# Reordering the loads, the weight conversions and the splits around the first groups of a fused attention and feed-forward kernel

## The chip, the cores and the metric

One core of one Trainium2 chip runs the whole program. The metric is the device time of one execution in microseconds (us), the median over repeated executions.

## The reference, cut to what matters

```python
# r, k, v, w: (4, 8, 768, 48) fp32; u: (8, 48); moe weights arrive as 64-bit floats
for t in range(S):                       # linear attention, a decaying state of 48x48 per batch and head
    cur = u * kt (x) vt
    y[:, :, t] = rt . (state + cur)
    state = wt * state + kt (x) vt
x = y.transpose(0, 2, 1, 3).reshape(3072, 384)
h = max(x @ w1, x @ w2, x @ w3)          # 384 -> 768, elementwise maximum of three products
out = h @ w_out                          # 768 -> 384
```

## The kernel before, in words

**Attention.** The 768 steps of each of the 4 batches are cut in 6 chunks of 128 steps, 24 chunks in all, k = 0 to 23, worked in order with all 8 heads together. Each chunk runs through steps that a letter names: `n` loads its transposed inputs (tile `tin`, three buffers), `b` and `f` are two scans on VectorE, `r` three multiplications on VectorE, `d` and `D` and `e` make the diagonal term (for chunks from 6 on `d` is two GpSimd multiplications and a VectorE sum; `e` ends in two GpSimd selects), `X` is the scores on TensorE, `M` the masked copy of the scores by VectorE, `T`, `R`, `U`, `V`, `Z` are small TensorE stages, `S` the new state, `c` a check on ScalarE (a square, summed), `E` copies the result to `x` and, at the third and fourth chunk of a half, issues DMAs inside SBUF that move 16 rows (`x<-x`, L570). X, V, U and Z of a chunk come together; the text calls that stretch on TensorE the chunk's visit. V needs M of the same chunk.

**Layer.** The 3072 tokens are six halves of 512. Half h takes chunks 4h to 4h+3. A half has 18 groups, here G0 to G17 for the first half (three matrices times six column blocks of 128), and then eight out-steps, out0 to out7. In the first half, G0 to G5 multiply in plain fp32 (one term); from G6 on each product is split in a high and a low part, three matmul terms for each of three row blocks: `x_hi*wh`, `x_lo*wh`, `x_hi*wl`. So G6 and on need the split of x (`x_hi` by ScalarE, then `x_lo` by VectorE) and the split of their weight (`wh` by ScalarE, then `wl` by VectorE). The out-steps of the first half are plain fp32. The product of a group lies in one of three PSUM buffers (`psm`) until it is taken up: by a ScalarE copy (L132) for the first of three matrices, by a VectorE maximum (L135) for the other two. G0 and G1 are begun on the first three chunks' columns and ended on the fourth's.

**Weights.** There are 24 weight blocks of 128 rows, 0 to 17 for the groups, 18 to 23 for the second product. A block i goes through: a load by SP's queue into a ring of six `raw` buffers (`load_w`); a cast on ScalarE (`split_w1`, tile `top`, L311); a VectorE instruction that joins the halves to fp32 (`split_w2`, L318); and the split of it (`split_w3`: `wh` on ScalarE L112, and `wl` on VectorE L113, issued one call of `fix` later). A load into a `raw` buffer waits until the VectorE instruction that read the block six before it is over.

**Order.** The schedule is written out by hand: every engine works its instructions in the order in which this code issues them. `FRONT` is a list of steps for chunks 0 to 4 (two characters: a step and its chunk; one character: an action). `START` goes on with actions alone, and then a loop does the rest: there `group()` issues the next group and `unit()` the next sixth of a chunk's visit. The actions: `w` load the next weight block, `i` cast the next one, `c` cast ahead and join the next one (`weights`), `f` split the next one in `ORDER` (6 to 17, then 0 to 5, then 18 to 23) and issue the `wl` of the one before it (`fix`), `y` split the next third of x (`x_next`), `p` and `m` the next group, `a` the next unit of attention. `W3` stands for three idle matmuls. `begin` also loads ahead, up to `NST` blocks past the one being cast.

Of the kernel before, what the change touches and what calls it, by code (L numbers as in the profile page):

```python
# [62 lines left out]
GPH = 3 * FT + 2 * CPH  # L63
UPC = 6
UPH = UPC * CPH
NST = 3
WARM = 10
XD, LEAD = -2, 0

FRONT = ("b0 s0 f0 d0 W2 D0 W3 r0 X0 e0 T0 W3 c0 b1 s1 d1 D1 U0 f1 W2 R0 e1 S0 O0 V0 Z0 E0 n3 r1 "
# [3 lines left out]
TURN = "b1 d1 w | f1 w | D1 r1 c1 | e1 M0 w | "  # L76
ORD = "w R0 V0 U0 X1 Z0 E0 N1 b2 d2 | f2 n3 w | D2 S0 r2 c2 | e2 M1 w | T1 w | |"


START = ("mcyamcyfamcyffamcfamcfamcfaamcfamcfaamcfamcfaamcfamcfaamcfamccaamccamcaaamfamfmfamxfamamfmamf")  # L80
CS = 6
EARLY = 2
LINE = 128
# [12 lines left out]
def kernel(ctx: ExitStack, tc, tin, nat, u_flat, u_pair, v_t, w_all, out, ytr):  # L96
# [13 lines left out]
    def split(hi, lo, src, later=None):  # L110

        nc.scalar.copy(out=hi, in_=src)  # L112
        rest = lambda: nc.vector.tensor_tensor(out=lo, in0=src, in1=hi.bitcast(F32), op=ALU.subtract)  # L113
        rest() if later is None else later.append(rest)
# [90 lines left out]
    with ExitStack() as fast:  # L205
# [88 lines left out]
        def load_w():  # L294
            nonlocal loaded
            if loaded == NW:
                return
            i, loaded = loaded, loaded + 1
            if w_all.dtype == F32:
                place(i)  # L300
                nc.sync.dma_start(out=wval[i], in_=w_all[i])
                return
            raw = raw_p.tile([128, lines(2 * PC + 1)], I32, name="raw")
            nc.sync.dma_start(out=raw[:, :].bitcast(U16)[:, 1:4 * PC + 1], in_=w_all[i].bitcast(U16))
            stage[i] = raw
# [7 lines left out]
        def split_w2(i):  # L313

            if w_all.dtype == F32:
                return
            place(i)
            nc.vector.scalar_tensor_tensor(out=wval[i].bitcast(U32), in0=stage.pop(i)[:, 1:2 * PC:2].bitcast(U32), scalar=13,  # L318
                                           in1=tops[i % 3][:, :], op0=ALU.logical_shift_right, op1=ALU.bitwise_or)
# [12 lines left out]
        def split_w3(i):  # L332

            whi[i] = hi_p.tile([128, PC], F32R, name="wh")[:, :]
            wlo[i] = lo_p.tile([128, PC], F32R, name="wl")[:, :]
            split(whi[i], wlo[i], wval[i], wrest)
# [240 lines left out]
        def ahead(step, k):  # L577

            if k < NK and (step, k) not in ready:
                ready.add((step, k))  # L580
                steps[step](k)
# [63 lines left out]
        def begin():  # L645

            nonlocal begun
            while loaded < min(NW, begun + (NST if groups else 1)):
                load_w()
            if begun < NW:  # L650
                split_w1(begun)
                begun += 1

        def weights():

            nonlocal done
            if done == NW:
                return
            while begun < min(NW, done + 2):
                begin()  # L660
            split_w2(done)
            done += 1

        ORDER = [*range(3 * SPLIT, 3 * FT), *range(3 * SPLIT), *range(3 * FT, NW)]
# [10 lines left out]
        def fix():  # L675

            nonlocal fixed
            flush_one = wrest.pop(0) if wrest else None
            if fixed < NW:
                split_w3(ORDER[fixed])  # L680
            if flush_one:
                flush_one()
            fixed += 1
# [46 lines left out]
        def group():  # L730
# [25 lines left out]
            while fixed < due(half, g):  # L756
                fix()
# [8 lines left out]
        def part():  # L766
# [3 lines left out]
            next(mg)  # L770

        simple = dict(p=part, a=unit, c=weights, i=begin, w=load_w, m=group, f=fix, y=x_next, x=lambda: take_x(True))
        for step in FRONT.split():
            if step in simple:
# [3 lines left out]
            else:  # L778
                ahead(step[0], int(step[1:]))
        for step in START:  # L780
            simple[step]()
# [7 lines left out]
    with tc.If(verdict[0] != 0, label="general"), ExitStack() as slow:  # L789
        pool = lambda name, bufs, **kw: slow.enter_context(tc.tile_pool(name=name, bufs=bufs, **kw))  # L790
        c1 = pool("c1", 1)
# [83 lines left out]
        with tc.For_i(0, NH) as half:  # L875
            x = xs_p.tile([128, KT, HT], F32, name="x")
# [73 lines left out]
```

## Time and profile before

| | |
|---|---|
| median of 3 runs | 412.01 us (411.22 to 412.81) |
| the profiled execution, its own time | 415.78 us |
| its span in the trace | 414.0 us |
| mean granted TensorE clock | 0.984 of full |
| busy: TensorE / VectorE / ScalarE / GpSimd | 397.9 / 253.6 / 177.9 / 82.7 us |

All times in the trace are microseconds from the start of the span, in the profiled execution. An engine name in a row is PE (TensorE), DVE (VectorE), ACT (ScalarE), POOL (GpSimd) or SP; a trailing q is the engine's queue of DMA issues. In a timeline row the first number is the start, the second the duration (of all that a row merges), and what stands in brackets is how long the engine was idle ahead of it and what ended that. Durations of neighbouring instructions on an engine overlap by about a tenth of a microsecond, so the time that one takes in a queue is read from start to start. A plain fp32 matmul leaves two records, so six records are one plain group.

### The profile page before, as it was taken

Reading aid. Unit: us, or ns where it says so; the run is one execution under the profiler, and the core shown is the slowest. Engines: PE = TensorE matmul, PEld = TensorE weight load, DVE = VectorE, ACT = ScalarE, POOL = GpSimd, SP = SyncE. Lnnn points to the kernel's source line nnn. Section 1 sums busy time; section 2 is a strip of 40 time slices with the busy share of each in tenths; the row PEclk is TensorE's granted clock in tenths of the full one; section 3 lists DMA queues with packets and bytes.
Section 4 is the critical chain, followed back from the end, with each engine's and each line's share of the span. In section 5 each row is a group of like instructions: output and inputs, shape, how many; then the busy total and the mean of one; then the engine's idle time right before and its main releaser. Section 6 shows DMA issues by size and latency. Waiting matters only on the chain.

```text
span 414.0 us, 9214 instructions
## 1 busy us (share of the span) xinstructions
PE 397.9 (96%) x3762; PEld 322.8 (78%) x3762; DVE 253.6 (61%) x440; ACT 177.9 (43%) x403; POOL 82.7 (20%) x95
## 2 busy tenths in 40 slices
PE   6997999798999999999999999999999999999995
PEld 2665467675688888988888988889988888978895
DVE  7975789979737858457658558667656532233320
ACT  2854465454524323546545746644623421412211
POOL 3220013235221421311321311322222200000000
PEclk9998799989999999999999999999999999999998
DMA  8766974760540412380330370430460000300002
GB/s 214 210 180 200 351 240 143 246 195 9 175 161 5 126 31 96 74 273 4 123 96 30 81 268 2 149 101 0 141 206 2 2 2 0 97 1 2 1 0 80
DMA packets 20814, 44.65 MB, mean 108 GB/s; under 512 B 2944, under 2 KB 9536, under 8 KB 20768
## 3 DMA queue, kind: packets, MB, share of 16 engines
q1 hardware_dynamic: 20160, 43.34, 33.8%
q10 hardware_dynamic: 608, 0.69, 0.5%
q8 instruction: 30, 0.49, 0.5%
q14 instruction: 16, 0.13, 0.1%
HBM read 38.12 MB, written 4.72 MB: 103 GB/s over the span
## 4 chain that ended last, share of the span: by engine, by line
PE 88%; DVE 4%; ACT 2%; DMA 2%; issue 2%; ACTq 1%; SPq 1%; POOL 0%; POOLq 0%; DVEq 0%
PE psm L169 51%; PE psm L189 19%; PE gram L451 4%; PE y L543 4%; PE tu L504 3%; PE y L494 3%; PE psm L594 2%; PE tu L481 2%; DMA raw<-in_w_all_dram 2%; DVE wl L113 1%; DVE gf L355 1%; PE psm L406 1%; DVE h_hi L135 1%; ACTq L570 1%; SPq L570 1%
## 5 line engine op out<-in xcount | busy, mean ns | idle before, releaser
L169 PE MATMUL psm<-x_hi,wh 128*128 128x512 f32 x306 | 122.6, 401 | 2.1 <-ACT h_hi L132 2.1
L169 PE MATMUL psm<-x_hi,wl 128*128 128x512 f32 x306 | 120.1, 393 | 0.1
L169 PE MATMUL psm<-x_lo,wh 128*128 128x512 f32 x306 | 119.8, 392 | 0.0
L135 DVE TENSOR_TENSOR m<-psm,m 128x512 f32<-128x512 f32 x60 | 41.5, 691 | 72.8 <-PE psm L169 59.9
L169 PEld LDWEIGHTS psm<-x_hi,wh 128*128 128x128 f32 x306 | 57.6, 188 | 14.9 <-ACT h_hi L132 2.3
L169 PEld LDWEIGHTS psm<-x_hi,wl 128*128 128x128 f32 x306 | 57.7, 189 | 13.0 <-DVE wl L113 0.8
L169 PEld LDWEIGHTS psm<-x_lo,wh 128*128 128x128 f32 x306 | 57.8, 189 | 11.4 <-DVE x_lo L113 0.2
L430 POOL TENSOR_SCALAR_AFFINE_SELECT a<-cs 64x512 f32<-64x512 f32 x44 | 31.4, 714 | 135.3 <-DVE cs L421 62.9
L189 PE MATMUL psm<-wl,h_hi 128*128 128x384 f32 x168 | 56.2, 379 | 0.0
L396 POOL TENSOR_TENSOR kr<-kr 128x384 f32<-128x384 f32 x18 | 25.2, 1399 | 108.5 <-PE y L543 100.4
L561 ACT COPY x<-y 112x512 f32<-112x512 f32 x24 | 14.0, 584 | 67.8 <-PE y L543 67.8
L189 PE MATMUL psm<-wh,h_hi 128*128 128x384 f32 x120 | 41.0, 342 | 0.0
L189 PE MATMUL psm<-wh,h_lo 128*128 128x384 f32 x120 | 40.3, 335 | 0.0
L112 ACT CAST h_hi<-m 128x512 fp32r<-128x512 f32 x30 | 18.7, 622 | 47.8 <-DVE m L135 47.8
L189 PEld LDWEIGHTS psm<-wl,h_hi 128*128 128x128 f32 x168 | 31.5, 188 | 5.9
L385 ACT ACTIVATE gf<-gf 112x1034 f32<-112x1034 f32 x24 | 25.6, 1067 | 20.6 <-DVE tin L380 20.6
L113 DVE TENSOR_TENSOR h_lo<-m,h_hi 128x512 fp32r<-128x512 f32 x30 | 20.7, 690 | 21.8 <-ACT h_hi L112 21.8
L368 DVE TENSOR_TENSOR_SCAN gf<-tin,d_fwd 112x517 f32<-112x517 f32 x24 | 33.2, 1382 | 0.7
L355 DVE TENSOR_TENSOR_SCAN gf<-tin,d_bwd 112x517 f32<-112x517 f32 x24 | 30.2, 1260 | 2.8 <-DMA tin<-in_tin_dram 2.8
L543 PE MATMUL y<-a,v 64*48 64x64 f32 (+3 forms) x768 | 25.4, 248 | 2.6 <-issue 1.9
L543 PEld LDWEIGHTS y<-a,v 64*64 64x64 f32 (+1 forms) x768 | 21.4, 128 | 6.3 <-issue 4.5
L132 ACT COPY m<-psm 128x512 f32<-128x512 f32 x30 | 17.4, 581 | 18.6 <-PE psm L169 12.8
(87 smaller groups left out, 500.2 us busy)
## 6 DMA issues: line engine op xcount, KB each, us to landing
tin<-in_tin_dram SPq DMA_DIRECT2D x23, 448.0 KB, 4.6
raw<-in_w_all_dram SPq DMA_DIRECT2D x24, 384.0 KB, 4.6
kr<-in_nat_dram SPq DMA_DIRECT2D x18, 384.0 KB, 4.8
tin<-in_tin_dram SPq DMA_DIRECT2D x23, 231.0 KB, 3.0
v<-in_nat_dram SPq DMA_DIRECT2D x24, 192.0 KB, 4.6
out_dram<-m SPq DMA_DIRECT2D x23, 192.0 KB, 2.1
x<-x SPq DMA_DIRECT2D x30, 32.0 KB, 2.0
tin<-in_tin_dram SPq DMA_DIRECT2D x1, 256.0 KB, 4.5
```

The source lines that it names most:

```text
L112: nc.scalar.copy(out=hi, in_=src)
L113: rest = lambda: nc.vector.tensor_tensor(out=lo, in0=src, in1=hi.bitcast(F32), op=ALU.subtract)
L132: nc.scalar.copy(out=top["m"][:, :], in_=ps[:, :])
L135: nc.vector.tensor_tensor(out=m[:, :], in0=ps[:, :], in1=m[:, :], op=ALU.max)
L169: nc.tensor.matmul(ps[:, :], lhsT=wt[f * 3 + wi][:, ct * 128:(ct + 1) * 128], rhs=xt[:, ct, :], start=(n == 0), stop=(n == KT * len(terms) ...
L189: nc.tensor.matmul(pss[tt][:, 0:DM], lhsT=ht[f][:, tok], rhs=wt[FT * 3 + f][:, :], start=(f == 0 and i == 0), stop=(f == FT - 1 and i == l ...
L355: nc.vector.tensor_tensor_scan(out=gf[0:112, 0, ::-1], data0=t[0:112, 0:WC][:, ::-1], data1=d_bwd[0:112, ::-1], initial=0.0, op0=ALU.mult, ...
L368: nc.vector.tensor_tensor_scan(out=gf[0:112, 1, :], data0=tbuf[k % NB][0:112, 0:WC], data1=d_fwd[0:112, :], initial=0.0, op0=ALU.mult, op1 ...
L385: nc.scalar.activation(out=flat, in_=flat, func=AF.Square, accum_out=acc[0:112, k:k + 1])
L396: nc.gpsimd.tensor_tensor(out=n[:, 0, :], in0=n[:, 0, :], in1=n[:, 1, :], op=ALU.mult)
L430: nc.gpsimd.affine_select(out=a[rows, 0:2, :, :], pattern=[[0, 2], [0, 4], [1, HC]], in_=cs[rows, :].rearrange("p (a b) -> p a b", a=2).un ...
L543: mm = nc.tensor.matmul(p["y"][64 * half:64 * half + m, hh, j, HC * late:C], lhsT=natt[k][0][lo:lo + HC, h * D:h * D + m], rhs=a[:, j, :] ...
```

## The change

It rewrites `FRONT` from the second line on and `START`, sets `NST` from 3 to 5, and lets `fix` join the weight block that it splits where that isn't done yet.

```diff
-NST = 3
+NST = 5
...
-         "W1 X1 d2 D2 e2 w w T1 c1 b2 s2 R1 U1 S1 O1 V1 Z1 E1 f2 r2 "
-         "W4 X2 d3 D3 e3 w n4 w T2 c2 b3 s3 R2 U2 S2 i i O2 V2 Z2 E2 f3 r3 "
-         "W3 X3 T3 i R3 O3 x V3 Z3 E3 w w n5 U3 p p d4 w c n6 w m D4 b4 s4 c c3 S3 m w f4 c e4 m r4 c X4 N4 T4 R4 c4 w w")
+         "W1 X1 d2 D2 e2 w w w w T1 c1 b2 s2 R1 U1 S1 O1 V1 Z1 E1 f2 r2 "
+         "W4 X2 d3 D3 e3 n4 w w T2 c2 b3 s3 R2 U2 S2 i i O2 V2 Z2 E2 f3 r3 "
+         "W3 X3 T3 i R3 O3 x V3 Z3 E3 U3 p p d4 c n5 w w m D4 b4 s4 c3 S3 y c w w m f4 e4 y c m r4 y c f X4 N4 T4 R4 c4 w w n6")
...
-START = ("mcyamcyfamcyffamcfamcfamcfaamcfamcfaamcfamcfaamcfamcfaamcfamccaamccamcaaamfamfmfamxfamamfmamf")
+START = ("mcfamcfamcfamcfamcfaamcfaamcfamcfaamcfamcfaamcfamccaamccamcaamfamfamfamxfmamfmamf")
...
             if fixed < NW:
+                while done <= ORDER[fixed]:
+                    weights()
                 split_w3(ORDER[fixed])
```

Read out, block by block: weight blocks 2 and 3 are loaded two blocks earlier in SP's order, blocks 4 and 5 ahead of the DMAs `x<-x` of chunks 2 and 3 instead of behind them; the loads of `tin` for chunks 5 and 6 come later among the weights. ScalarE casts block 4 after the check and the state of chunk 3 instead of before. x's three splits and the join of blocks 5 to 7 are issued between G0 and G3 instead of from G3 to G6, and the split of each weight from block 6 on about one group earlier. The visits of chunks 5 and 6 come after G10 and G14 (before: after G11 and G15), that of chunk 7 after out1 (before: after out0). The `wl` of block 17 is issued on VectorE behind M of chunk 7, just ahead of G17 (before: between G15 and G16, ahead of the scans of chunk 8). x's splits for the second half are issued at out2, ahead of the check of chunk 9 (before: at out4, behind it). From G1 of the second half on the order is the one of before.

## Rows read from the trace of the kernel before

**Rows 1.** PE's timeline from the end of G1 to the end of G5.
```profile
36.46 0.94 PE L157 MATMUL psm<-x,wh 128*128 128x128 f32 x6
40.07 5.49 PE L169 MATMUL psm<-x,wh 128*128 128x512 f32 x6 [2.67 <-ACT h_hi L132]
45.49 1.14 PE L451 MATMUL gram<-tin 48*64 48x128 f32 x32
...
47.68 7.99 PE L169 MATMUL psm<-x,wh 128*128 128x512 f32 x18
```
**Rows 2.** Windows: busy of PE, PEld, DVE, ACT, POOL, then granted clock, DMA share, GB/s.
```profile
40.00:42.00 2.00, 1.93 (x3) 0.90 (x4) 1.95 (x3) 0.57 (x3) 1.31 (x2) 0.50 1.08 289
...
84.00:85.00 1.00, 1.00 (x4) 0.81 (x3) 1.00 (x3) 0.78 (x3) 0.00 (x0) 0.50 0.00 0
```
**Rows 3.** ACT's timeline from 33 to 40 us.
```profile
33.78 0.62 ACT L311 CAST top<-raw 128x384 f16<-128x384 bf16 x1 [2.60 <-DMA x<-x]
...
37.14 0.62 ACT L311 CAST top<-raw 128x384 f16<-128x384 bf16 x1 [2.69 <-DMA raw<-in_w_all_dram]
37.64 1.05 ACT L385 ACTIVATE gf<-gf 112x1034 f32<-112x1034 f32 x1
...
39.42 0.60 ACT L132 COPY h_hi<-psm 128x512 f32<-128x512 f32 x1
```
**Rows 4.** The timeline of SP's queue in the same stretch.
```profile
26.91 6.58 SPq L570 DMA_DIRECT2D x<-x  x6
33.54 1.05 SPq L304 DMA_DIRECT2D raw<-in_w_all_dram  x2
```
**Rows 5.** One window: from `r` of chunk 4 to `M` of chunk 7 on DVE.
```profile
40.66:97.84 57.18, 53.28 (x470) 36.03 (x468) 48.90 (x84) 29.84 (x64) 14.03 (x15) 0.92 0.66 217
```
**Rows 6.** DVE's timeline: single instructions out of that window.
```profile
42.28 0.68 DVE L380 TENSOR_TENSOR tin<-tin,gf 112x512 f32<-112x512 f32 x1
...
73.54 1.36 DVE L113 TENSOR_TENSOR wl<-wl,wh 128x384 fp32r<-128x384 f32 x1
74.82 2.04 DVE L355 TENSOR_TENSOR_SCAN gf<-tin,d_bwd 112x517 f32<-112x517 f32 x1
...
77.84 0.55 DVE L113 TENSOR_TENSOR wl<-wl,wh 128x384 fp32r<-128x384 f32 x1
...
86.27 1.22 DVE L355 TENSOR_TENSOR_SCAN gf<-tin,d_bwd 112x517 f32<-112x517 f32 x1
...
97.21 0.72 DVE L466 COPY_PREDICATED a<-mask,gram 128x512 f32<-128x512 int32 x1
```
**Rows 7.** POOL's timeline: the `d` multiplications of chunks 7 and 8.
```profile
73.11 1.38 POOL L396 TENSOR_TENSOR kr<-kr 128x384 f32<-128x384 f32 x1 [0.96 <-PE y L543]
74.56 1.21 POOL L397 TENSOR_TENSOR kr<-kr,u_bc 128x384 f32<-128x384 f32 x1
...
87.44 1.37 POOL L396 TENSOR_TENSOR kr<-kr 128x384 f32<-128x384 f32 x1 [3.50 <-PE y L543]
```
**Rows 8.** PE's timeline from G15 to the second half's first group.
```profile
82.78 0.50 PE L169 MATMUL psm<-x_hi,wh 128*128 128x512 f32 x1 [2.07 <-ACT h_hi L132]
...
86.26 0.89 PE L543 MATMUL y<-a,v 64*64 64x128 f32 x16
...
93.06 2.10 PE L189 MATMUL psm<-wl,h_hi 128*128 128x384 f32 x6
...
98.02 0.56 PE L543 MATMUL y<-a,v 64*64 64x128 f32 x16 [1.89 <-issue]
...
100.27 9.94 PE L189 MATMUL psm<-wl,h_hi 128*128 128x384 f32 x30
...
114.02 0.69 PE L169 MATMUL psm<-x_hi,wh 128*128 128x512 f32 x1
```
**Rows 9.** The chain that ended last: start, length, what; the stretch after 114 us.
```profile
367.87 28.81 PE psm L169 x126
```
**Rows 10.** SP's queue: the DMAs `x<-x` after chunk 7.
```profile
101.03 4.04 SPq L570 DMA_DIRECT2D x<-x  x6
```

More of the change, by code (lines that the diff above doesn't have):

```diff
@@ L72 @@
 FRONT = ("b0 s0 f0 d0 W2 D0 W3 r0 X0 e0 T0 W3 c0 b1 s1 d1 D1 U0 f1 W2 R0 e1 S0 O0 V0 Z0 E0 n3 r1 "
[3 rows of a table removed]
[3 rows of a table added]
 TURN = "b1 d1 w | f1 w | D1 r1 c1 | e1 M0 w | "
 ORD = "w R0 V0 U0 X1 Z0 E0 N1 b2 d2 | f2 n3 w | D2 S0 r2 c2 | e2 M1 w | T1 w | |"
-START = ("mcyamcyfamcyffamcfamcfamcfaamcfamcfaamcfamcfaamcfamcfaamcfamccaamccamcaaamfamfmfamxfamamfmamf")
+START = ("mcfamcfamcfamcfamcfamcfaamcfamcfaamcfamcfaamcfamcfaamcfamccaamccamcaamfamfamfamxfmamfmamf")
 CS = 6
```

## The prediction

> **What bounds the kernel now.** I read the chain of waits first. From the second half's first group, at 114.0 us, to the end it is TensorE at one rate: 126 matmuls in 28.81 us, 0.229 each [rows 9]. The change doesn't reorder that stretch, so what it is worth is how much earlier the first matmul of half 1 starts than 114.02 [rows 8]. Ahead of it the timeline of TensorE shows where time is lost; the reader is to look for idle time in brackets, and for a group that takes twice its usual time.
>
> First loss: G1 ends at 37.40 and G2 starts at 40.07, 2.67 us idle, and takes 5.49 us; G3 to G5, same shape, take 7.99, 2.66 each [rows 1]. In the window at 40 us the granted clock is 0.50, 1.2 GHz, in place of 2.4 [rows 2]. So this place costs 2.7 + 2.8. ScalarE's timeline says why: G2 needs the copy at 39.42, which stands behind the check and the state of chunk 3, and those behind the cast of block 4 at 37.14, which waited 2.69 us for its load [rows 3]. SP's queue says why the load was late: it was issued at 33.54, behind six x DMAs that waited for chunks 2 and 3 [rows 4].
>
> Second loss: 2.07 us idle ahead of G15 at 82.78, after which its nine matmuls take 3.48 us (to 86.26) instead of 2.06 [rows 8], clock again 0.50 [rows 2]. Third: 1.89 us ahead of V of chunk 7 at 98.02 [rows 8], which needs M of chunk 7, ended at 97.84 on VectorE [rows 5, 6]. Both come from one engine: between 40.66 and 97.84 VectorE is busy 48.90 of 57.18 us [rows 5]. It is the second bound of this stretch, and its 8.3 us idle is nearly as much as TensorE loses.
>
> **The change part by part.** *Loads of blocks 2 to 5 earlier.* The number of DMAs is the same. Blocks 4 and 5 leave SP's queue before the six x DMAs start at 26.91 [rows 4], so the 2.69 us wait for the load [rows 3] goes. ScalarE's own order then is: cast of block 3 at 33.78 as before, to 34.4 with a small copy; check and state of chunk 3, 1.8 (37.64 to 39.42 before), to 36.2; the new x_hi, 0.5, to 36.7; cast of block 4, 0.5 (37.14 to 37.64), to 37.2; the copy for G2, 0.5, to 37.7 [rows 3]. G2 starts at 37.8 rather than 40.07, idle 0.4, and I expect the clock to stay up, since no gap of that size is followed by 0.50 in these rows; if it falls, 2.8 more (5.49 less 2.66 [rows 1]). x_hi and its x_lo go into time that both engines wait in now: nothing, as long as the copy isn't late. `NST` 5 makes SP wait for the buffer ring at blocks 10 and 13, with chunk 6's inputs behind block 13; that wait ends with the join of block 7 near 44, and the scan that needs those inputs comes past 55: nothing.
>
> *What is late next.* After the copy VectorE takes up G1 (0.6) and starts `r` of chunk 4 at 38.5, not 40.66. It takes 2.2 (to the end of the row at 42.28 [rows 6]), so X of chunk 4 starts near 40.7; X, T, R take 2.2 as from 45.49 to 47.68 [rows 1], and G3 starts at 42.9: 4.8 us ahead. TensorE then has the same work as before from 47.68 to the gap before G15 (80.71), 33.0 us, and chunk 6's visit and G15, G16 behind it, 2.25 (98.02 to 100.27 [rows 8]) and 18 matmuls of 0.229 [rows 9], 4.1: it would reach G17 at about 82.3.
>
> *VectorE's queue.* Its work from `r` of chunk 4 to the `wl` of block 17 is what it did in the window, 48.90 [rows 5], with these differences: one x_lo is done earlier, 0.6 (start to end of a like row, 42.28 [rows 6]); taking up G16 now comes later, 0.6; and the `d` of chunk 8 on GpSimd, which ran from 87.44 [rows 7] where VectorE stood idle, now falls where VectorE is busy. The price of that is read at chunk 7: GpSimd's two instructions at 73.11 and 74.56 [rows 7], and under them a `wl` of 1.36 beside 0.55 alone, and a scan of 2.04 beside 1.22 [rows 6]: 1.6 together. Sum 48.9 - 0.6 - 0.6 + 1.6 = 49.3, and with no idle time left the `wl` of block 17 ends at 38.5 + 49.3 = 87.8. The change puts it behind M of chunk 7; G17's third matmul needs it. So TensorE stands from 82.3 or so to 87.8, over 5 us: the stalls at G2, G15 and V of chunk 7 are gone and a longer one comes at G17. For `d` of chunk 8 nothing is the lower bound (it may meet instructions that it doesn't hold up: end at 86.2). The upper one is all of 1.38 + 1.21 [rows 7], and I add 0.5 for idle time that remains on VectorE: 89.3. I take 1.6, the one pair of rows where it is seen.
>
> The Trainium skill, "SBUF — State Buffer", section "Who interferes with whom", says that a VectorE instruction with two SBUF inputs and a GpSimd instruction that reads SBUF contend, and that the later one waits until the first is over. Rows 6 and 7 agree that they contend, with 0.8 us for each in place of a whole GpSimd instruction. By the rule this visit costs up to 2.6 instead of 1.6, and the saving below would be 1.8 instead of 2.8; it speaks against putting VectorE's idle time to use under GpSimd.
>
> *From G17 on.* Seven matmuls remain, 1.6 [rows 9]. A stall of 5 us is longer than either that was followed by a clock of 0.50, so I charge a fall: 1.7 as at G15 (3.48 less 2.06, and V's 0.82 less about 0.5 [rows 8]) to 2.8 as at G2 [rows 1], taken as 2.3. Then T, R and the visit of chunk 7 and the eight out-steps: from out0 at 93.06 to 114.02 less the 1.89 idle, 19.1 [rows 8]. Moving the visit behind out1 changes only the order. x's splits for half 1 now stand on ScalarE ahead of the copy of the first output tile, and they wait for the DMAs that take SP 4.04 us to issue [rows 10]. I estimate that the copy comes 7.4 us after the visit, where TensorE needs its buffer after four steps of the visit's successors at about 7.0: 0.4, between 0 and 1.6.
>
> *Sum.* 87.8 + 1.6 + 2.3 + 19.1 + 0.4 = 111.2 for the first matmul of half 1, against 114.0: 2.8 us saved. On the profiled execution's own 415.8 (span 414.0 and 1.8 around it) that is 413.0; the median shown is 3.8 lower, so 412.0 - 2.8 = 409.2. With the bounds: 86.2 + 1.6 + 1.7 + 19.1 = 108.6, 5.4 saved, to 89.3 + 1.6 + 2.8 + 19.1 + 1.6 = 114.4, 0.4 lost: 406.6 to 412.4.
>
> **The rivals.** *All of it comes back.* If VectorE's queue isn't what holds G17 (its work being shorter than the window's sum, or the `wl` early enough), G17 ends at 84.4 and half 1 starts at 84.4 + 19.1 + 0.4 = 103.9: 10 saved, 402. For it: 8.3 us of VectorE's idle time in the window, and TensorE's losses add up to about that. Against it: the sum of the queue, in which 5 us would have to be missing. With half of them missing it is 405.
>
> *The early part doesn't come off.* Either the loads don't land sooner, or the clock falls at G2 all the same. G2 at half rate delays G3 to G5 by 2.8, VectorE waits for them, and G17 with it: 2.8 - 2.5, about 412, no change. For it: the DMA engines' share is 1.08 at 40 us [rows 2], though that is where these loads leave from; and the gap before G2 still is 0.4.
>
> *Slower.* GpSimd holds VectorE up longer. 14.03 us of GpSimd work lie in the window [rows 5]. If each of the three `d` visits, all now under a busy VectorE, cost the whole 2.6, and the selects as much as they last, the `wl` of block 17 would end at 93 or later. From 92.7 on (4.9 past 87.8) the kernel is more than 0.5% slower: about 414.5 at 93. Against it: in the same rows the contention is 1.6 for a whole visit, and it is in the 48.9 for two of the three.
>
> **How the numbers follow.** My forecast has 0.61, the whole or half of the gain 0.13, no early gain 0.18, slower 0.08. 0.5% is 2.1 us, about what a measurement of this kernel can tell from no change. Of the forecast, two thirds lie beyond 2.1 us saved (0.41) and the rest within it (0.20). So faster is 0.41 + 0.13 = 0.54, same 0.20 + 0.18 = 0.38, slower 0.08. The likeliest time is 409.2, its own range 406.6 to 412.4. The range that holds 8 in 10 goes to 404.0, halfway into the first rival, and to 413.0, so as to hold the second: left out are about 0.08 below and 0.08 above.
>
> **What would show it.** ScalarE's cast of block 4 without a wait for its load; G2 at about 37.8 and in 2.7 us; X of chunk 4 near 41 and G3 near 43; no idle time before G15 beyond 1 us and none before V of chunk 7; VectorE without idle time from 38.5 to 88; and then G17 split in two, two matmuls before and seven after a gap of some 5 us that ends with the `wl` of block 17 near 87.8, clock 0.50 behind it. I am wrong if that gap is missing (then the gain is over 5 us), if G2 still runs at 1.2 GHz, or if the stretch from out0 to half 1 holds a new wait of over 2 us.

## The result, and the profile after

The changed kernel takes 407.3 us (median of 4 runs, 406.0 to 408.1) against 412.4 of the kernel before (411.2 to 413.5) beside it: ratio 0.9874, 95% interval 0.9835 to 0.9913. A second measurement later gave 406.8 against 412.7, 0.9868 (0.982 to 0.9915). The span of the profiled execution fell from 414.0 to 406.4 us.

**A correction first.** The `START` in the section on the change is not that of the kernel that ran. In copying it two pieces `mcfa` were lost, and the reading of the order behind it and the prediction went by the short one. The right line is:

```diff
+START = ("mcfamcfamcfamcfamcfamcfaamcfamcfaamcfamcfaamcfamcfaamcfamccaamccamcaamfamfamfamxfmamfmamf")
```

By it the visits of chunks 5 and 6 stay behind G11 and G15, as before; the `wl` of block 17 is issued between G14 and G15, three groups ahead of M of chunk 7, which stands behind G17; and x's splits for the second half stay at out4. What was said of `FRONT`, of `NST`, of `fix` and of chunk 7's visit behind out1 holds. The order that the prediction reasoned about was run as a kernel of its own, below.

TensorE's timeline after, which answers to [rows 1, 8]:

```profile
37.97 2.84 PE L169 MATMUL psm<-x,wh 128*128 128x512 f32 x6 [0.18 <-ACT h_hi L132]
...
42.69 7.99 PE L169 MATMUL psm<-x,wh 128*128 128x512 f32 x18
...
76.75 0.50 PE L169 MATMUL psm<-x_hi,wh 128*128 128x512 f32 x1 [1.89 <-ACT h_hi L132]
...
80.57 0.56 PE L543 MATMUL y<-a,v 64*64 64x128 f32 x16
...
87.03 2.10 PE L189 MATMUL psm<-wl,h_hi 128*128 128x384 f32 x6
...
91.97 0.56 PE L543 MATMUL y<-a,v 64*64 64x128 f32 x16
...
106.25 0.47 PE L169 MATMUL psm<-x_hi,wh 128*128 128x512 f32 x1
```

G2 waits 0.18 us instead of 2.67 and takes 2.84 instead of 5.49. The gap before G15 is still there, 1.89 us. V of chunk 7, at 91.97, has no idle time ahead of it. Half 1 starts at 106.25 instead of 114.02, 7.8 us earlier, and the rest of the span is as long as before (300.2 and 300.0 us).

Windows after (columns as in [rows 2]): the clock stays at 1.00 where it was 0.50 at 40 us, and is again below 1 behind G15's gap.

```profile
40.00:44.00 4.00, 4.00 (x57) 2.25 (x56) 4.00 (x8) 3.13 (x6) 0.00 (x0) 1.00 1.04 398
76.00:80.00 4.00, 3.25 (x8) 2.57 (x9) 4.00 (x8) 3.82 (x10) 1.31 (x2) 0.64 0.87 262
```

ScalarE after, against [rows 3], and further down the check of chunk 7:

```profile
36.81 0.66 ACT L311 CAST top<-raw 128x384 f16<-128x384 bf16 x1
37.31 0.60 ACT L132 COPY h_hi<-psm 128x512 f32<-128x512 f32 x1
...
75.06 1.07 ACT L385 ACTIVATE gf<-gf 112x1034 f32<-112x1034 f32 x1 [2.63 <-DVE tin L380]
...
76.12 0.57 ACT L132 COPY h_hi<-psm 128x512 f32<-128x512 f32 x1
```

The cast of block 4 (36.81) doesn't wait, and G2's copy follows at once. The last two rows explain G15's gap: the copy that frees a product buffer stands behind the check of chunk 7, which waited 2.63 us for VectorE's `r` of chunk 7.

VectorE after, which answers to [rows 6]:

```profile
38.64 1.21 DVE L379 TENSOR_TENSOR tin<-tin,gf 112x256 f32<-112x256 f32 x2
...
78.23 0.55 DVE L113 TENSOR_TENSOR wl<-wl,wh 128x384 fp32r<-128x384 f32 x1
...
84.98 0.56 DVE L318 SCALAR_TENSOR_TENSOR wl<-raw,top 128x384 uint32<-128x384 uint32 x1 [3.07 <-ACT top L311]
...
91.15 0.72 DVE L466 COPY_PREDICATED a<-mask,gram 128x512 f32<-128x512 int32 x1
```

`r` of chunk 4 starts at 38.64 (40.66 before), the `wl` of block 17 is over at 78.7, and M of chunk 7 (91.15) just in time for V at 91.97.

### The profile page after: what moved, and what is told of

Same layout as the page of the kernel before. It is cut to its first block, busy times and chain, and to the rows that moved or that the text cites. A ratio compares the mean times of both kernels' runs of the same rounds, so it can differ in the third digit from the quotient of the medians.

```text
span 406.4 us, 9216 instructions
## 1 busy us (share of the span) xinstructions
PE 394.4 (97%) x3762; PEld 322.2 (79%) x3762; DVE 252.9 (62%) x440; ACT 177.9 (44%) x403; POOL 79.7 (20%) x95
## 4 chain that ended last, share of the span: by engine, by line
PE 88%; DVE 4%; ACT 2%; issue 2%; ACTq 1%; DMA 1%; POOL 0%; SPq 0%; POOLq 0%; DVEq 0%
PE psm L169 51%; PE psm L189 19%; PE gram L451 4%; PE y L543 4%; PE tu L504 3%; PE y L494 3%; PE psm L594 2%; PE tu L481 2%; ACTq L570 1%; DVE wl L113 1%; DMA v<-in_nat_dram 1%; PE psm L406 1%; DVE gf L368 1%; DVE h_hi L135 1%; DVE gf L355 0%
## 5 line engine op out<-in xcount | busy, mean ns | idle before, releaser
L396 POOL TENSOR_TENSOR kr<-kr 128x384 f32<-128x384 f32 x18 | 23.5, 1308 | 108.1 <-PE y L543 100.7
L355 DVE TENSOR_TENSOR_SCAN gf<-tin,d_bwd 112x517 f32<-112x517 f32 x24 | 31.1, 1295 | 3.3 <-DMA tin<-in_tin_dram 3.3
L132 ACT COPY m<-psm 128x512 f32<-128x512 f32 x30 | 17.4, 581 | 19.2 <-PE psm L169 14.6
L113 DVE TENSOR_TENSOR x_lo<-x,x_hi 128x512 fp32r<-128x512 f32 x18 | 11.5, 688 | 21.4 <-ACT x_hi L112 21.4
```

The source lines that it names most:

```text
L132: nc.scalar.copy(out=top["m"][:, :], in_=ps[:, :])
L355: nc.vector.tensor_tensor_scan(out=gf[0:112, 0, ::-1], data0=t[0:112, 0:WC][:, ::-1], data1=d_bwd[0:112, ::-1], initial=0.0, op0=ALU.mult, ...
L396: nc.gpsimd.tensor_tensor(out=n[:, 0, :], in0=n[:, 0, :], in1=n[:, 1, :], op=ALU.mult)
```

## The experiments

All times are medians beside runs of the kernel before on the same chip. Of each profile I took the start of G0's first matmul and four stages of TensorE behind it, in us: A from there to G3, B from G3 to G15, C from G15 to out0, D from out0 to half 1. The kernel before appears twice, the changed one and the check a unit later too.

```
                               G0     A      B      C      D     A-D    time, and ratio to before
before, first profile        31.27  16.41  35.10  10.28  20.96  82.75   412.0
before, again                31.01  15.32  35.10   8.74  21.10  80.26   413.0
visit alone                  30.68  13.04  35.11  10.25  19.75  78.15   411.9  0.9988 (0.9939-1.0038)
order on ScalarE alone       30.39  11.33  36.62  10.25  20.95  79.15   412.1  0.9991 (0.9957-1.0025)
loads alone                  32.13  10.70  35.09   8.73  21.10  75.62   410.0  0.9937 (0.9896-0.9978)
front alone                  31.81  10.64  33.11   8.74  22.73  75.22   408.9  0.9907 (0.9869-0.9944)
order as read                31.33  10.67  36.37  11.70  19.86  78.60   411.4  0.9957 (0.9922-0.9991)
changed, loads late          30.91  10.98  35.27  10.25  19.22  75.72   407.8  0.9880 (0.9820-0.9940)
changed                      31.65  11.04  34.06  10.28  19.22  74.60   407.3  0.9874 (0.9835-0.9913)
changed, again               31.28  10.59  34.02   8.74  19.34  72.69   406.8  0.9868 (0.9820-0.9915)
check a unit later           31.73  11.05  31.95  10.19  20.14  73.33   406.5  0.9843 (0.9786-0.9900)
check a unit later, again    31.45  10.78  31.95  10.18  20.14  73.05   406.0  0.9840 (0.9793-0.9887)
check behind T               31.53  10.98  31.94   9.54  20.82  73.28   405.7  0.9826 (0.9781-0.9872)
```

Two things in the table bear on every comparison. The first three rows have the same code up to G3, and their A is 16.41, 15.32 and 13.04: what the change saves there depends on the execution. And G0 starts at 30.39 to 31.27 in the five profiles with the loads of before, at 31.28 to 32.13 in the eight with early loads, on average 0.8 us later: the early loads have a price ahead of A, for which the prediction has no term. ScalarE's issue of chunk 2's three DMAs `x<-x`, which stands ahead of G0, takes 2.2 to 2.7 us in the five and 2.4 to 3.4 in the eight; that this is the way was not tried.

The theory that I tested: the gain is G2's wait for block 4 (A), VectorE's work moved into idle time (B), and V of chunk 7's wait (D). The rival: VectorE's queue takes part of it back at another place.

**The kernel before, once more.** No edit.

> The kernel before, unchanged, profiled once more. Its first profiled execution took 415.8 us and its timed runs 411.2 to 413.5; the first profile saves 7.6 us of span against the changed kernel, the medians 5.1. If a stall of the first profile was that execution's own, the span is near 410 to 411 and one of three places is milder: G2's wait and half clock (2.7 + 2.8), the gap before G15 and the half clock behind it (2.1 + 1.7), V of chunk 7 (1.9). If the stalls belong to the kernel, the span is near 414 again.

It took 413.0 us with a span of 411.3. TensorE's timeline:

```profile
39.91 4.54 PE L169 MATMUL psm<-x,wh 128*128 128x512 f32 x6 [2.77 <-ACT h_hi L132]
...
81.43 0.50 PE L169 MATMUL psm<-x_hi,wh 128*128 128x512 f32 x1 [2.06 <-ACT h_hi L132]
...
95.27 0.56 PE L543 MATMUL y<-a,v 64*64 64x128 f32 x16 [2.03 <-issue]
```

The three gaps are there again; the half clock behind them is not the same. G2 takes 4.54 us instead of 5.49, and behind G15's gap there is no half clock: C is 8.74 instead of 10.28. That accounts for 2.5 of the 2.7 us between the two spans. So 7.6 us saved between the first two profiles overstates the change.

**The front alone.**

```diff
 (the changed kernel)
-START of the changed kernel
+START of the kernel before
```

> The changed kernel with the START of before: early loads, NST 5, joins and x's splits early, but chunk 7's visit behind out0 as before. Theory (the early part carries the gain, the visit's move adds what V of chunk 7 waited): G2 near 38, G3 near 42.7, G15 near 77, and V of chunk 7 waits again for M, 1 to 2 us: 1.0 to 1.9 us slower than the changed kernel, about 409. Rival (the visit's move is idle once VectorE is ahead): no wait, as fast as the changed kernel.

```profile
75.56 0.50 PE L169 MATMUL psm<-x_hi,wh 128*128 128x512 f32 x1 [0.94 <-ACT h_hi L132]
...
89.40 0.56 PE L543 MATMUL y<-a,v 64*64 64x128 f32 x16 [2.03 <-issue]
```

The theory holds in the profile: V of chunk 7 waits 2.03 us, and here the clock falls behind that wait (D 22.73, 1.6 more than 21.10). The time is 1.4 us above the changed kernel's by the ratios, with intervals that overlap.

**The visit alone.**

```diff
 (the kernel before, in START)
-mcaaamfam
+mcaamafam
```

> The kernel before with one edit: chunk 7's visit behind out1 instead of out0. Theory: M of chunk 7 ends as before near 97.8, out1 fills the 1.9 us wait, 1.5 to 1.9 us faster than before, about 410.5. Rival (the work that stands behind the visit becomes late in its turn, the copies of x and the x DMAs first): the wait comes back at out5 or at half 1, under 0.5 us faster.

```profile
38.84 2.84 PE L169 MATMUL psm<-x,wh 128*128 128x512 f32 x6 [2.02 <-ACT h_hi L132]
...
92.84 1.56 PE L189 MATMUL psm<-wl,h_hi 128*128 128x384 f32 x4 [0.38 <-DVE wl L318]
```

V's wait is gone and D is 1.35 shorter, with a new wait of 0.38. The time moved by 0.6 us with an interval that holds both theory and rival: not settled by the clock, and the profile leans to the theory. The first row brought something else: G2's gap of 2.02 without a half clock behind it.

**The loads alone.**

```diff
 (the kernel before)
-... e2 w w T1 ...      e3 w n4 w T2 ...      E3 w w n5 U3 ...
+... e2 w w w w T1 ...  e3 n4 w w T2 ...      E3 n5 U3 ...
```

> The kernel before with one edit: weight blocks 2 to 5 loaded earlier as in the change, all else (NST 3, x's splits, joins, visits) as before. Theory (the late load of block 4 is the cause of G2's wait and of the half clock behind it): the cast of block 4 waits no longer, G2 starts near 38 in 2.7 us, G3 4 to 5 us earlier; then x's third split, still issued at G5, and VectorE's queue decide: 2.5 to 5 us faster than before. Rival (the loads alone give it back because VectorE, with x's splits and the wl's late, is the bound from G6 on): G2 early, but G15 no more than 1.5 us earlier, 410.5 to 412.

2.6 us faster by the ratio, at the low end of the theory, with an interval (0.9 to 4.3) that reaches into the rival. G15 comes at 77.92, against 82.78, 81.43 and 78.83 in the three profiles whose code up to there is that of before: 3.1 us earlier on average, which leans to the theory, though against the last it is only 0.9. A falls to 10.70 as in the changed kernel, but B stays 35.09 and D 21.10: two of the three gaps are untouched.

```profile
77.92 0.49 PE L169 MATMUL psm<-x_hi,wh 128*128 128x512 f32 x1 [2.06 <-ACT h_hi L132]
91.75 0.56 PE L543 MATMUL y<-a,v 64*64 64x128 f32 x16 [2.03 <-issue]
```

From here to the front alone the early joins and splits, `NST`, ScalarE's order and the later loads of `tin` are added: B falls by 2.0. Which of them does it was not tried one by one.

**The changed kernel with the loads late again.**

```diff
 (the changed kernel)
-... e2 w w w w T1 ...  e3 n4 w w T2 ...      E3 U3 ...
+... e2 w w T1 ...      e3 w n4 w T2 ...      E3 w w U3 ...
```

> The changed kernel with the order of the loads of weight blocks 0 to 5 put back (blocks 4 and 5 behind the x DMAs again). Theory: the wait for block 4 returns, now with x's first split ahead of it on ScalarE: G2 near 40, 2 to 2.5 us idle and perhaps half clock; 2 to 5 us slower than the changed kernel. Rival (x's split and the check fill that time, so that the load is hidden): under 0.7 us slower.

The rival holds for the time: 0.2 us more than the changed kernel by the ratios, less than can be told. But the late loads do cost something in the profile. ScalarE's rows show that the cast that waits is now that of block 6, 3.54 us, behind G2's copy and x's splits; VectorE waits 2.23 us for it, and TensorE 0.27 at G6 for x_lo:

```profile
36.05 0.63 ACT L311 CAST top<-raw 128x384 f16<-128x384 bf16 x1
...
42.24 0.62 ACT L311 CAST top<-raw 128x384 f16<-128x384 bf16 x1 [3.54 <-DMA raw<-in_w_all_dram]
```

```profile
42.90 0.56 DVE L318 SCALAR_TENSOR_TENSOR wl<-raw,top 128x384 uint32<-128x384 uint32 x1 [2.23 <-ACT top L311]
```

```profile
52.53 0.50 PE L169 MATMUL psm<-x_lo,wh 128*128 128x512 f32 x1 [0.27 <-DVE x_lo L113]
```

B is 35.27 instead of 34.06, 1.2 longer (G15's gap is 2.32 instead of 1.89). G0 starts 0.74 earlier in return, and half 1 at 106.63 instead of 106.25, so in the profiles most of the loss is given back ahead of A.

**The order on ScalarE alone.** So is the order on ScalarE enough?

```diff
 (the kernel before)
-D4 b4 s4 c c3 S3 m
+D4 b4 s4 c3 S3 c m
```

> The kernel before with one edit on ScalarE: the check and the state of chunk 3 ahead of the cast of weight block 4 instead of behind it, the loads left late. Theory (it is the order on ScalarE, not the load, that makes G2 wait: with the loads late again the changed kernel lost nothing): the cast of block 4 waits less, G2 starts near 38 in 2.7 us, as with the loads alone 2 to 4 us faster than before. Rival (the load is the cause): G2 still near 40, under 1 us faster.

My expectation of the time failed. G2's wait does go (0.31), against the rival, but the time is that of before. TensorE and ScalarE:

```profile
36.83 2.84 PE L169 MATMUL psm<-x,wh 128*128 128x512 f32 x6 [0.31 <-ACT h_hi L132]
...
53.38 0.50 PE L169 MATMUL psm<-x_lo,wh 128*128 128x512 f32 x1 [0.92 <-DVE x_lo L113]
```

```profile
42.29 0.63 ACT L311 CAST top<-raw 128x384 f16<-128x384 bf16 x1 [4.68 <-DMA raw<-in_w_all_dram]
```

The wait for loads moved to a later cast, 4.68 us, and here x's splits stand behind it: G6 waits 0.92 us for x_lo, and B is 1.5 longer. In the changed kernel x_hi and two of the three x_lo stand ahead of that cast, and late loads cost G6 0.27 instead of 0.92. A and B together are 47.95 here, and 51.51, 50.42 and 48.15 in the three profiles with the code of before: where the clock stays up behind G2's gap, the order alone saves next to nothing.

**The order that the prediction read.**

```diff
 (the changed kernel)
-START of the changed kernel
+START as printed in the section on the change
```

> The order that the prediction worked with: its START lacks one piece (m, c, f, a) and one more of the changed kernel's, so that the visits of chunks 5 and 6 come a group earlier and the wl of block 17 stands on VectorE behind M of chunk 7. The prediction's sum: that wl ends at 87.8 (86.2 to 89.3), G17 stands split after two matmuls for 5 us, the clock falls, half 1 starts near 111.2: 409.2 us, so 2 us slower than the changed kernel. Rival (VectorE's work is shorter than the window's sum, since less of GpSimd's work meets it): the wl by 84, the gap under 2 us, as fast as the changed kernel.

411.4 us, ratio 0.9957 (0.9922 to 0.9991): it gives back most of the gain. Its VectorE and TensorE:

```profile
38.25 0.75 DVE L379 TENSOR_TENSOR tin<-tin,gf 112x256 f32<-112x256 f32 x2
...
85.07 0.72 DVE L466 COPY_PREDICATED a<-mask,gram 128x512 f32<-128x512 int32 x1
85.68 0.69 DVE L113 TENSOR_TENSOR wl<-wl,wh 128x384 fp32r<-128x384 f32 x1
```

```profile
82.85 0.39 PE L169 MATMUL psm<-x_lo,wh 128*128 128x512 f32 x1
86.43 0.80 PE L169 MATMUL psm<-x_hi,wl 128*128 128x512 f32 x1 [3.19 <-DVE wl L113]
87.02 0.63 PE L169 MATMUL psm<-x_hi,wh 128*128 128x512 f32 x1
87.45 0.63 PE L169 MATMUL psm<-x_lo,wh 128*128 128x512 f32 x1
...
104.99 4.78 PE L189 MATMUL psm<-wl,h_hi 128*128 128x384 f32 x14 [0.89 <-ACT m L200]
```

G17 is split after two matmuls. VectorE went from 38.25 to 86.4, 48.1 us, for what I had counted as 38.5 to 87.8, 49.3; the gap is 3.6 us from start to start where I had over 5, the clock falls behind it (0.43 from start to start in place of 0.229; granted clock 0.53 from 86.4 to 90.0), and out5 waits 0.89 for a copy. G15 has no gap, but the visit ahead of it, chunk 6's, waits 0.69 and 1.18 us.

**The check a unit later.** This takes away what is left before G15.

```diff
 (the changed kernel, ORD)
-| D2 S0 r2 c2 | e2 M1 w | T1 w | |
+| D2 S0 r2 | e2 M1 c2 w | T1 w | |
```

> The changed kernel with one edit in every chunk's units from chunk 4 on: the ScalarE check (c) stands a unit later, behind e and M instead of behind r. Theory: what is left before G15 (1.9 us idle, then nine matmuls in 3.8 instead of 2.06 us at 1.2 GHz) comes from the copy that frees G12's buffer, which stands on ScalarE behind the check of chunk 7, and that waits for VectorE's r of chunk 7. With the check behind, the copy comes 3 us earlier, G15 follows T without a gap at 2.4 GHz: 3 to 3.7 us faster than the changed kernel, near 404. Rival (VectorE is the bound there: its wl and M come just as late): the gap moves to G15's third matmul or to V of chunk 6, 0 to 1.5 us faster.

406.5 us, 0.9843 (0.9786 to 0.99). G15 follows T without a gap, so the copy behind the check was the cause; but the size was wrong, about 1 us, as the rival had it: 2.2 us come back at chunk 6's visit and at out1 (the repeat's expectation calls it out2; it is the second matmul of out1, ahead of chunk 7's visit), the latter a place that I had not named. The second row below is U of chunk 6, which waits for ScalarE's copy of T, not far behind the check now.

```profile
77.80 0.56 PE L543 MATMUL y<-a,v 64*64 64x128 f32 x16 [0.78 <-POOL a L430]
...
78.94 0.67 PE L504 MATMUL tu<-v,kn 128*64 128x48 f32 x16 [0.59 <-ACT kn L483]
...
88.86 1.56 PE L189 MATMUL psm<-wl,h_hi 128*128 128x384 f32 x4 [0.80 <-DVE wl L318]
```

**Three versions on one chip.** The changed kernel, the check a unit later, and the check behind T (`| D2 S0 r2 | e2 M1 w | T1 c2 w | |`).

> The changed kernel, unchanged, beside the next three on one chip. 406 to 408 us. If the half clock behind G15 comes and goes from one execution to the next, its second profile may lack it: span then about 405 in place of 406.4.

> The changed kernel with the check a unit later, again, for the comparison on one chip. Its first profile had no gap before G15, 1.4 us of new waits at chunk 6's visit and 0.8 at out2. Expected 1.0 us faster than the changed kernel; the rival is that what it saves before G15 is all given back, under 0.3.

> As the one before, but the check stands one unit later still, behind T. Theory: in the first version the copy of chunk 6's T stood on ScalarE behind the check and held up U of chunk 6 by 0.6 us; now it does not: 0.3 to 0.6 us faster than with the check a unit later. Rival: the visit then waits 0.6 us more at another place (M of chunk 6, the select), no difference.

406.8 (405.5 to 408.0), 406.0 (405.2 to 407.5) and 405.7 us (404.6 to 406.1). The last is the fastest kernel here, 0.9826 of before (0.9781 to 0.9872); against the changed kernel the order is as expected, but the runs overlap. With the check behind T the wait of U is gone, as the theory has it, but that at out1 is 1.07 instead of 0.80, and A to D are 73.28 against 73.05 with the check a unit later: between these two neither the times nor the profiles settle it. The second profile of the changed kernel lacks the half clock behind G15:

```profile
75.89 0.50 PE L169 MATMUL psm<-x_hi,wh 128*128 128x512 f32 x1 [1.84 <-ACT h_hi L132]
...
78.15 0.56 PE L543 MATMUL y<-a,v 64*64 64x128 f32 x16
```

With nearly the same gap as in the first, its nine matmuls take 2.26 us there (granted clock 1.00 from 75.9 to 79.0) and 3.82 in the first profile (0.60 from 76.7 to 81.0), and the span is 403.8 instead of 406.4.

## Why the prediction came out as it did

The time lies within the range (404.0 to 413.0), and the sign is right; the saving is 5.1 to 5.9 us where the sum said 2.8. That the number came out near is in part luck: the stall that the sum rests on isn't in the kernel that ran, and other losses that the sum had taken away stayed. Step by step:

- *The load of block 4 no longer holds ScalarE, G2 at 37.8 with full clock:* right, 37.97 and 2.84. Against the second profile of before, A shrank by 4.3, against the visit alone by 2.0. But "the loads" were only one of two ways to that: with the loads late and ScalarE's order new, G2 starts as early. What the prediction left out is where the wait goes then, to the cast of a later block, which holds up VectorE's join, and x's splits where they stand behind it; and that early loads put back G0.
- *`r` of chunk 4 at 38.5, G3 at 42.9:* 38.64 and 42.69.
- *A stall at G17 of over 5 us, and 2.3 for the clock behind it:* this is the step that failed, and it failed in the reading of `START`. The kernel that ran has the `wl` of block 17 over at 78.7, before TensorE needs it at G17, so there is neither the stall nor the clock behind it. By the sign that the prediction gave (wrong if that gap is missing, and then the gain is over 5 us) the forecast did not come true; what ran is the first rival's condition, the `wl` early enough, without the rival's full gain. Where the order is the one that I had read, the stall is there, at the matmul that I named, but smaller than counted: 3.6 us long with the `wl` at 86.4 (bounds 86.2 to 89.3), since of the 1.6 charged for `d` of chunk 8 the rows show about 1.0 (a scan of 2.04 at 77.60, two joins of 1.20 at 80.14 against 1.04 at 76.64). The seven matmuls behind it take 3.15 us instead of 1.6, so the clock cost about 1.5 where I had charged 2.3. Half 1 starts at 109.93 there (111.2 in the sum), and the time is 1.8 us below that of before by the ratio (2.8 in the sum).
- *The gap before G15 goes:* wrong, 1.89 us stay. I counted VectorE's queue but not ScalarE's copy behind the check, though that releaser stood in [rows 8]. Moving the check showed it.
- *VectorE without idle time until 88:* wrong with the same step; it idles 3.07 us until 84.98, since the casts stand on ScalarE behind the copy of chunk 6's result, which waits 3.14 us for TensorE. In the order as read it has one gap, of 0.72 us, from 38.25 to 86.4.
- *V of chunk 7 waits no longer:* right; D went from 21.1 to 19.2.
- *0.4 us at out5:* not in the changed kernel, where x's splits stay at out4; 0.89 in the order as read.
- *From the profiled execution to the median:* the sum took both half clocks, 2.8 and 1.7, as the kernel's own. They come and go, so part of what a profile saves isn't in the medians: 7.6 us of span, 5.1 and 5.9 of the medians.

The time lies between the forecast (409.2) and the half of the first rival (405). The stages as the second profile of before has them and the changed kernel's give 4.3 (A), 1.0 (B) and 1.9 (D), less 1.5 for a half clock in C that the one profile has and the other hasn't, and less 0.6 for the later start of G0: 5.0 us. Of B's gain, 2.0 in the front alone and 1.0 in the changed kernel, what causes it is not shown. Why G15's gap is 0.94 there and 1.89 here was not tried either; the traces point to GpSimd's visit of chunk 7, which stretches a `wl` and a scan of VectorE in the changed kernel (1.37 and 2.05 us) and a `wl` (1.37) but not the scan (1.25) in the front alone, ahead of the same `r` of chunk 7.

## What to carry to other kernels

When an engine's order is written by hand, follow each wait to the instruction that stands behind it: a wait for a load costs nothing until the copy or the split that another engine needs is queued behind it, and moving the instruction took away the wait at G2 as moving the load did. Alone it only handed the wait on to a later cast (412.1 us against 410.0 with the loads alone), so look for what stands behind that one too. A check or a sum that nobody waits for belongs behind the copies that free buffers, though here most of what that saved came back at the next waits. Take two profiles of the kernel before, so as not to charge one execution's half clock to the code. And copy an order by program, not by eye: the stall on which this prediction's sum rests came out of two lost pieces of a string.

## What the runs showed of the hardware

The half clock behind a short gap is not a property of the kernel alone: the same kernel shows it in one execution and not in another. Behind G15's gap of 1.8 to 2.3 us C is either 8.73 to 8.74 us (before again, loads alone, changed again, and the front alone with 0.94) or 10.25 to 10.28 (before, visit alone, order alone, changed, loads late). Behind G2's gap the clock fell after 2.67 and 2.77 us idle and did not after 2.02. One such fall is worth 1.5 us, 0.4% of this kernel, more than the visit alone or the order on ScalarE alone moved the time.

A GpSimd instruction beside them costs the `wl` and the scan 0.8 us each, after as before, and the rows show how. In the profile after, the `wl` at 67.49 and the scan at 68.79 each last until the GpSimd instruction beside them is over, and then 0.41 and 1.09 us, most of their own 0.55 and 1.22:

```profile
67.41 1.04 POOL L396 TENSOR_TENSOR kr<-kr 128x384 f32<-128x384 f32 x1 [1.31 <-PE y L543]
68.53 1.22 POOL L397 TENSOR_TENSOR kr<-kr,u_bc 128x384 f32<-128x384 f32 x1
```

```profile
67.49 1.37 DVE L113 TENSOR_TENSOR wl<-wl,wh 128x384 fp32r<-128x384 f32 x1
68.79 2.05 DVE L355 TENSOR_TENSOR_SCAN gf<-tin,d_bwd 112x517 f32<-112x517 f32 x1
```

The 0.8 us that the prediction took per instruction is about what remained of the GpSimd instruction when VectorE's came, 0.96 us both times; the 0.14 of difference is what VectorE's own time behind it falls short by. The rule that it weighed (the Trainium skill, "SBUF — State Buffer", section "Who interferes with whom": the later one waits until the first is over) fits these rows, and [rows 6, 7] already: there too the two end 0.41 and 1.09 us behind GpSimd's. The prediction was wrong to read them as less than the rule. In the front alone GpSimd's instruction comes while a `wl` of VectorE runs (66.93 to 67.50); there it is GpSimd's that is long, 2.29 us, and the scan of chunk 7 takes 1.25:

```profile
67.17 2.29 POOL L396 TENSOR_TENSOR kr<-kr 128x384 f32<-128x384 f32 x1 [1.64 <-PE y L543]
```

```profile
67.40 1.25 DVE L355 TENSOR_TENSOR_SCAN gf<-tin,d_bwd 112x517 f32<-112x517 f32 x1
```
